# Sums of squares of the weight blocks on TensorE instead of ScalarE, for blocks 4 to 15 of a three-layer kernel

## The chip, the cores and the metric

The kernel runs on one core of a Trainium2 chip. The metric is the device time of one execution in microseconds; the time before is 1081.05 us, the median of three runs (1079.14 to 1084.92). The core has five engines with a queue of instructions each: TensorE (PE; its loads of weights are shown apart as PEld), VectorE (DVE), ScalarE (ACT), GpSimd (POOL) and SyncE (SP), which issues most transfers. Each engine takes its queue in the order in which the program lists it, and waits on semaphores for the others.

## The reference

Three layers follow each other: an attention between tokens and a small state, a dense layer with a squared Relu, and a layer of eight experts of which each token takes one.

```
scores = x @ state.T / 8;  a = softmax(scores);  xread = a @ state        # x: 8 batches, 8 heads, 512 x 64
scores2 = state @ x.T / 8; a2 = softmax(scores2); sread = a2 @ x          # state: 32 x 64 per head
x = concat(xread, sread) as 4608 tokens of 512
h = x @ w_in;  x = relu(h)**2 @ w_out                                     # w_in 512 x 2048, w_out 2048 x 512
expert = argmax over 8 of cosine(x, expert_emb) / tau, gate = its softmax
out = gate * (relu(x @ w1[expert]) @ w2[expert])                          # w1 512 x 1024, w2 1024 x 512
```

The inputs w_in and w_out come as float64, that is as words of 8 bytes, and the kernel decodes them to float32 itself.

## The kernel before

**Weights.** w_in and w_out are read in 16 blocks of 128 x 1024 numbers, numbered 0 to 15 in the order in, in, out, out, in, in, out, out and so on (`BLOCKS`). A block of w_in is 256 of its 2048 columns, a block of w_out 256 of its 2048 rows. Block 4 is the third of w_in, and 4 to 15 hold six of each. A raw block lies in one of a few places (`RAW_IN`) that is used again for later blocks: block 10 goes where block 6 lay, block 15 where 12 lay.

`to_f32` decodes a block in three steps. ScalarE turns the upper words into a float16 tile, the *top* (L915; two tiles named rec take turns). ScalarE or VectorE copies the top into float32 (L922 or L925), by which of the two the planner holds less loaded. VectorE sets the lower bits into it by a shift and an or (L928). Then the squares are summed. For w_in, `wi_scale` has ScalarE square the block into a tile pjk (L947), four matmuls against ones add over the rows (L955, into a bank of ps_u), and VectorE takes the maximum over columns (L961); for each pair of blocks that gives a power of two as scale (swi). For w_out, `wo_square` squares on ScalarE with a running sum (L1006); all eight sums are needed for the scale of w_out (L1028 and after).

The float16 products work on pairs of a high and a low part. `wi_split` and `wo_split` make them of the float32 blocks with the scales (L993 and L1054 on ScalarE, L317 on VectorE).

**The first tokens.** The kernel starts on tokens before all weights are there. For batch 0, `first_state_w` multiplies the state by float32 blocks as they come (L668) and splits the result (L677, L317). `up1` makes the hidden values in units u of 256 tokens and steps c = 0 to 7 of 256 columns (L1395 to L1397; below: Up c=0 to c=7); step c = 2k and 2k+1 needs the blocks 2k and 2k+1 of w_in and their scale. `hidden` applies Relu and square on ScalarE (L1348, L1352). `down1` multiplies unit 0 by w_out in float32 (L1458; Down c=0 to 7), later units in float16 (L1479 to L1481). Batch 1's attention begins meanwhile with sums of squares of its tokens and its state (L463, L465, L471).

**What sets the order.** The program is written by a planner: each piece of work is a thread with a priority, which yields the engine it needs next and a duration that the source assumes. `Plan.run` takes, over all threads, the step that can start first, then the one with the lower priority number, and each engine's queue is the order in which it took them. TensorE's banks of accumulation are rings of two (ps_u for sums and Up, ps_t for small products). At a priority of 1.3 to 5, a TensorE step counts as ready 1.75 us later than planned; the threads of the blocks have about 1.

Of the kernel before, what the change touches and what calls it, by code (L numbers as in the profile page):

```python
# [41 lines left out]
BW = DFF // NB  # L42
# [6 lines left out]
EASE = 1.0  # L49
LOADER = 9  # L50
AHEAD = 5
PRIO_A0 = 0.8
PRIO_A1 = 1.25
PRIO_S0 = 1.1
ATT = (0, 1, 2, B, 3, 4, 5, 6, 7)
XE = 2
# [168 lines left out]
def act(n):  # L225
    return "act", 0.1 + 0.83e-3 * n


def dve(n):
    return "dve", 0.09 + 1.045e-3 * n  # L230
# [10 lines left out]
def pe(k, n):  # L241
    return "pe", k * max(0.025, 0.0005 + n * 0.4205e-3)
# [3 lines left out]
def moe_kernel(  # L246
# [17 lines left out]
    nc = tc.nc  # L264
    ctx.enter_context(tc.manual_schedule())
    plan = Plan()
# [15 lines left out]
    att = ctx.enter_context(tc.tile_pool(name="att", bufs=1, side="right"))  # L282
# [54 lines left out]
    def load(dst, src, nbytes):  # L337
# [32 lines left out]
    smin, ismin = ends[:, 0:2], ends[:, 2:4]  # L370
# [23 lines left out]
    wi32 = [(wi_t[:, q + 1].rearrange("p h k f -> p (h k f)") if q < NB - 1 else  # L394
             wo[0].rearrange("p a k d -> p (a k d)")).bitcast(F32).rearrange("p (k f) -> p k f", k=4) for q in range(NB)]
# [5 lines left out]
    def ev(*key):  # L401
        return evs.setdefault(key, Ev(plan))
# [489 lines left out]
    top_slots = Ring(plan, 2)  # L892
    tops = [mg.tile([128, REC], F32, name=f"rec{k}", bufs=1)[:, :512].bitcast(BF16) for k in (4, 5)]

    def to_f32(n, dst, squares, squared):

        raw = raws.pop(n)
        slots = raw_in[RAW_IN[n]][0]
        over = [m for m in range(n) if RAW_IN[m] == "wo8"] if BLOCKS[n] in (("o", NB - 2), ("o", NB - 1)) else []
        if not W64:  # L900
            w = raw.bitcast(F32)
            plan.add(squares(w), plan.cur[1])
            for m in over:
                yield ev("read", m)
            yield dve2(1024)
            V.tensor_copy(dst, w)
        else:
            raw = raw.rearrange("p (n two) -> p n two", two=2)
            at = plan.now()
            yield top_slots  # L910
            plan.cur[2] = max(at, plan.now())
            k_t = top_slots.last()
            top = tops[k_t % 2]
            yield act(1024)
            nc.scalar.activation(out=top.bitcast(F16), in_=raw.bitcast(BF16)[:, :, 2], func=AF.Copy)  # L915
            at = plan.now()
            for m in over:
                yield ev("read", m)
            plan.cur[2] = max(at, plan.now())
            if plan.load("act") < plan.load("dve"):  # L920
                yield act(1024)
                nc.scalar.copy(dst, top)  # L922
            else:
                yield dve2(1024)
                V.tensor_copy(dst, top)  # L925
            top_slots.release(k_t)
            yield dve(1100)
            V.scalar_tensor_tensor(out=dst.bitcast(I32), in0=raw[:, :, 0], scalar=13, in1=dst.bitcast(I32),  # L928
                                   op0=ALU.logical_shift_right, op1=ALU.bitwise_or)
            plan.add(squares(dst), plan.cur[1])  # L930
            squared = ev("raw", n)
        plan.add(freed(n, slots, squared), plan.cur[1])

    def freed(n, slots, squared):
        yield squared
        ev("read", n).set()
        slots.release()

    wv = {}

    def wi_scale(q, w):
        at = plan.now()
        yield pjk_slots
        plan.cur[2] = max(at, plan.now())
        sq = att.tile([128, 4, BW], BF16, name="pjk")
        yield act(1024)
        nc.scalar.activation(out=sq, in_=w.rearrange("p (k f) -> p k f", k=4), func=AF.Square)  # L947
        ev("wisq", q).set()
        at = plan.now()
        yield u_slots  # L950
        plan.cur[2] = max(at, plan.now())
        p, k_h = ps_u.tile([128, 512], F32, name="u"), u_slots.last()
        yield pe(4, BW)
        for k in range(4):
            mm(p[:, 0:BW], lhsT=oneb, rhs=sq[:, k, :], start=k == 0, stop=k == 3)  # L955
        pjk_slots.release()
        if q // 2 not in wv:
            wv[q // 2] = small.tile([128, 2], F32, name="wv")
        v = wv[q // 2]
        yield dve(BW)  # L960
        V.tensor_reduce(out=v[:, q % 2:q % 2 + 1], in_=p[:, 0:BW], axis=X, op=ALU.max)  # L961
        u_slots.release(k_h)
        ev("wv", q).set()
        if q % 2:
            yield ev("wv", q - 1)
            qs = slice(q - 1, q + 1)
            yield tiny(5)
            w = small.tile([128, 4], F32, name="p2m")[:, 0:2]
            V.tensor_scalar(out=w, in0=v, scalar1=v[:, 0:1], scalar2=v[:, 1:2], op0=ALU.max, op1=ALU.max)
            v = w  # L970
            V.tensor_scalar(out=v, in0=v, scalar1=FLOOR, scalar2=None, op0=ALU.max)
            pow2(swi[:, qs], iswi[:, qs], v, 204)
            for a in (q - 1, q):
                ev("swi", a).set()
            yield ev("cg", 0)
            yield tiny(1)
            V.tensor_scalar(out=cgq[:, qs], in0=iswi[:, qs], scalar1=cg[:, 0:1], scalar2=None, op0=ALU.mult)
            ev("cgq", q // 2).set()

    def wi_block(n, q):  # L980
        yield ev("raw", n)
        yield from to_f32(n, wi32[q].rearrange("p k f -> p (k f)"), lambda a: wi_scale(q, a), ev("wisq", q))
        ev("wi32", q).set()
        plan.add(wi_split(q), PRIO_SPLIT)

# [11 lines left out]

    woacc = small.tile([128, NB], F32, name="woacc", bufs=1)

    def wo_square(q, w):  # L1000
        at = plan.now()
        yield pjk_slots
        plan.cur[2] = max(at, plan.now())
        jk = att.tile([128, 1024], BF16, name="pjk")
        yield act(1024)
        nc.scalar.activation(out=jk, in_=w, func=AF.Square, accum_out=woacc[:, q:q + 1])  # L1006
        pjk_slots.release()
        ev("wosq", q).set()

    def wo_block(n, q):  # L1010
        yield ev("raw", n)
        yield from to_f32(n, wo32[q].rearrange("p k d -> p (k d)"), lambda a: wo_square(q, a), ev("wosq", q))
        ev("f32", q).set()

    def weights():

        for n in range(1, len(BLOCKS)):
            if n == AHEAD:
                for t in range(2):
                    yield ev("asked", t)  # L1020
            yield from block(n)
            if n == LOADER:
                ev("w_in asked").set()
        for q in range(NB):
            yield ev("wosq", q)
            yield ev("swi", q)
        yield tiny(2)
        V.tensor_reduce(out=smin[:, 0:1], in_=swi, axis=X, op=ALU.min)  # L1028
        V.tensor_reduce(out=ismin[:, 0:1], in_=iswi, axis=X, op=ALU.max)
        yield from tensor_scale(woacc, smin[:, 1:2], ismin[:, 1:2])  # L1030
# [26 lines left out]
        split_lo(wo[q][:, 1], w, swo[:, q:q + 1], wo[q][:, 0])  # L1057
        ev("wo", q).set()

    def tensor_scale(acc, s, inv):  # L1060
# [12 lines left out]
        V.tensor_scalar(out=w, in0=p[:, 0:1], scalar1=FLOOR, scalar2=None, op0=ALU.max)  # L1073
        t_slots.release()
        pow2(s, inv, w, 204)

# [861 lines left out]
```

## Time and profile before

| | |
|---|---|
| Median of three runs | 1081.05 us |
| Profiled execution | 1085.53 us, span of its instructions 1083.7 us |
| TensorE matmuls busy | 1034.8 us, 95% of the span |
| VectorE busy | 669.9 us, 62% |
| ScalarE busy | 600.3 us, 55% |
| Granted TensorE clock, mean | 0.996 of 2.4 GHz |

Times in the rows are microseconds from the span's start unless marked ns. A row of the timeline shows the start, the time until the result is there, engine, line, operation, what it writes and reads and how often it stands there in a row, and in brackets how long the engine had been idle before and for whom. Matmuls overlap, so the time of one is longer than the distance to the next. A float32 matmul stands twice in the trace, and once in the program.

### The profile page before, as it was taken

Reading aid. Unit: us, or ns where it says so; the run is one execution under the profiler, and the core shown is the slowest. Engines: PE = TensorE matmul, PEld = TensorE weight load, DVE = VectorE, ACT = ScalarE, POOL = GpSimd, SP = SyncE. Lnnn points to the kernel's source line nnn. Section 1 sums busy time; section 2 is a strip of 40 time slices with the busy share of each in tenths; the row PEclk is TensorE's granted clock in tenths of the full one; section 3 lists DMA queues with packets and bytes.
Section 4 is the critical chain, followed back from the end, with each engine's and each line's share of the span. In section 5 each row is a group of like instructions: output and inputs, shape, how many; then the busy total and the mean of one; then the engine's idle time right before and its main releaser. Section 6 shows DMA issues by size and latency. Waiting matters only on the chain. (4 is left out here: it accounts for less than half of the span.)

```text
span 1083.7 us, 26223 instructions
## 1 busy us (share of the span) xinstructions
PE 1034.8 (95%) x10553; PEld 667.1 (62%) x10553; DVE 669.9 (62%) x1818; ACT 600.3 (55%) x1003; POOL 122.9 (11%) x149
## 2 busy tenths in 40 slices
PE   5789999899999999999999999999999999999998
PEld 4345465455565555656565666677676766767674
DVE  6779888778798877788887873465222222322222
ACT  6999898878887878879888783211111110101010
POOL 0000002002001001020010010321112111112111
PEclk9999999999999999999999999999999999999999
DMA  8843566755836655756766778834895767684792
GB/s 272 321 172 106 143 200 159 247 164 171 237 116 167 212 139 183 214 137 204 211 210 219 252 212 295 224 81 137 309 237 159 212 173 216 198 249 150 168 295 87
DMA packets 161599, 212.91 MB, mean 196 GB/s; under 512 B 112257, under 2 KB 115201, under 8 KB 156098
## 3 DMA queue, kind: packets, MB, share of 16 engines
q1 hardware_dynamic: 152722, 184.04, 58.1%
q0 software_dynamic: 8320, 27.08, 7.7%
q8 instruction: 84, 1.38, 0.5%
q14 instruction: 41, 0.34, 0.1%
q10 hardware_dynamic: 432, 0.08, 0.0%
HBM read 259.10 MB, written 51.68 MB: 287 GB/s over the span
## 5 line engine op out<-in xcount | busy, mean ns | idle before, releaser
L1745 ACT ACTIVATE r<-u 128x512 f32<-128x512 f32 x70 | 41.8, 597 | 323.3 <-PE u L1791 294.0
L1481 PE MATMUL d<-wo_t,g 128*128 128x512 f16 x512 | 194.1, 379 | 1.8 <-DVE g L1367 1.7
L1479 PE MATMUL d<-wo_t,g 128*128 128x512 f16 x512 | 194.0, 379 | 1.5 <-DVE g L1365 0.6
L1480 PE MATMUL d<-wo_t,g 128*128 128x512 f16 x512 | 194.0, 379 | 0.0
L1395 PE MATMUL u<-aT,sw 128*128 128x256 f16 x512 | 141.1, 276 | 7.7 <-ACT sw L677 4.3
L1397 PE MATMUL u<-aT,sw 128*128 128x256 f16 x512 | 140.8, 275 | 1.3 <-DVE sw L317 0.7
L1396 PE MATMUL u<-aT,sw 128*128 128x256 f16 x512 | 140.9, 275 | 0.5 <-issue 0.4
L1748 DVE CAST hh<-r 128x512 f16<-128x512 f32 x70 | 30.0, 429 | 137.3 <-ACT r L1745 135.8
L1348 ACT ACTIVATE r<-u,cg 128x512 f32<-128x512 f32 x128 | 87.5, 683 | 46.8 <-PE u L1397 22.8
L1759 DVE TENSOR_SCALAR o<-d,rec,wo_t 128x512 f32<-128x512 f32 x35 | 28.3, 809 | 107.6 <-PE d L1814 107.5
L1367 DVE TENSOR_TENSOR g<-r,g 128x512 f16<-128x512 f32 x128 | 87.7, 687 | 9.8 <-ACT r L1362 7.8
L1321 POOL DMA_INDIRECT rec_d<-rec,pi x34 | 37.6, 1105 | 494.0 <-DVE mt L774 91.2
L1814 PEld LDWEIGHTS <-hh 128*128 128x128 f16 (+1 forms) x688 | 54.6, 102 | 57.1 <-issue 0.4
L1481 PEld LDWEIGHTS <-g 128*128 128x128 f16 x512 | 50.0, 98 | 63.6 <-DVE g L1367 3.7
L1362 ACT ACTIVATE r<-r 128x512 f32<-128x512 f32 x128 | 80.2, 628 | 1.5
L1479 PEld LDWEIGHTS <-g 128*128 128x128 f16 x512 | 50.3, 98 | 49.2 <-DVE g L1365 1.1
L1480 PEld LDWEIGHTS <-g 128*128 128x128 f16 x512 | 50.1, 98 | 47.7 <-issue 0.9
L1789 PE MATMUL u<-xes,stage 128*128 128x128 f16 x448 | 76.1, 219 | 0.4 <-issue 0.4
L1790 PE MATMUL u<-xes,stage 128*128 128x128 f16 x448 | 76.1, 219 | 0.0
L1791 PE MATMUL u<-xes,stage 128*128 128x128 f16 x448 | 76.1, 219 | 0.0
L1395 PEld LDWEIGHTS <-sw 128*128 128x128 f16 x512 | 51.4, 100 | 33.0 <-issue 16.7
L1789 PE MATMUL u<-xes,xx 128*128 128x128 f16 x416 | 70.5, 219 | 0.0
(331 smaller groups left out, 2564.8 us busy)
## 6 DMA issues: line engine op xcount, KB each, us to landing
w_d<-he SPq DMA_DIRECT2D x128, 256.0 KB
g<-w_d SPq DMA_DIRECT2D x16, 2048.0 KB
wo_t<-w_d SPq DMA_DIRECT2D x16, 2048.0 KB
stage<-w_d SPq DMA_DIRECT2D x14, 2048.0 KB
he<-w_d SPq DMA_DIRECT2D x14, 2048.0 KB
xx<-w_d SPq DMA_DIRECT2D x13, 2048.0 KB
sw<-w_d SPq DMA_DIRECT2D x13, 2048.0 KB
stage<-in_w_dram SPq DMA_DIRECT2D x20, 1024.0 KB
```

Of the source, the lines that this page charges most:

```text
L1348: nc.scalar.activation(out=r, in_=ps, func=AF.Relu, scale=cg[:, g:g + 1] if u >= F32U else cgq[:, c:c + 1])
L1362: nc.scalar.activation(out=r, in_=r, func=AF.Square)
L1367: V.tensor_tensor(out=gl, in0=r, in1=gh, op=ALU.subtract)
L1395: mm(o, lhsT=hl[:, i, 0, fs], rhs=aT[:, i, :], start=i == 0, stop=False)
L1396: mm(o, lhsT=hl[:, i, 0, fs], rhs=aT[:, 2 + i, :], start=False, stop=False)
L1397: mm(o, lhsT=hl[:, i, 1, fs], rhs=aT[:, i, :], start=False, stop=i == 1)
L1479: mm(ps, lhsT=g_h[:, f, ts], rhs=w[:, 0, :], start=f == 0, stop=False)
L1480: mm(ps, lhsT=g_h[:, f, ts], rhs=w[:, 1, :], start=False, stop=False)
L1481: mm(ps, lhsT=g_l[:, f, ts], rhs=w[:, 0, :], start=False, stop=f == KF - 1)
L1789: mm(p[:, j, xs], lhsT=w[:, 0, k, fs], rhs=xe[:, k, xs], start=k == 0, stop=False)
L1790: mm(p[:, j, xs], lhsT=w[:, 0, k, fs], rhs=xe[:, 4 + k, xs], start=False, stop=False)
L1791: mm(p[:, j, xs], lhsT=w[:, 1, k, fs], rhs=xe[:, k, xs], start=False, stop=k == 3)
```

## The change

Blocks 4 to 15 (`GRAM`) no longer square their float32 form on ScalarE. As soon as a block's float16 top is there, TensorE multiplies each 128 x 128 piece of it by itself, eight matmuls into one 128 x 128 or two such sums; the sums of squares of the columns stand on the diagonals. VectorE multiplies by the unit matrix. For w_in a single matmul against ones in place of four then adds over the rows; for w_out VectorE adds over the columns. The top tile is given back after these products, and the raw place after the decoding. As tops are cut off below the exact number, the sums are multiplied by 1.14 and 1.13 before the power of two is taken. `PRIO_A1`, the priority of the attention threads of batches 1 to 8, is 1.24 for 1.25.

```
+GRAM = tuple(range(4, 16))
-PRIO_A1 = 1.25
+PRIO_A1 = 1.24
 # to_f32, after the top's conversion on ScalarE
+            gram = n in GRAM
+            if gram:
+                plan.add(squares(top, True), plan.cur[1])
...
+            if gram:
+                plan.add(topped(k_t, squared), plan.cur[1])
+            else:
+                top_slots.release(k_t)
+                plan.add(squares(dst, False), plan.cur[1])
+    def topped(k_t, squared):
+        yield squared
+        top_slots.release(k_t)
-    def wi_scale(q, w):
+    def wi_scale(q, w, gram):
+        if gram:
+            yield t_slots
+            p = ps_t.tile([128, 512], F32, name="t")[:, 0:BW].rearrange("p (c m) -> p c m", c=2)
+            w = w.rearrange("p (k c m) -> p k c m", k=4, c=2)
+            yield pe(8, 140)
+            for c in range(2):
+                for k in range(4):
+                    mm(p[:, c], lhsT=w[:, k, c], rhs=w[:, k, c], start=k == 0, stop=k == 3)
...
+        ks = 1 if gram else 4
+        if gram:
+            yield dve(BW)
+            V.tensor_tensor(out=sq.rearrange("p k (c m) -> p (k c) m", c=2), in0=p,
+                            in1=ident16.unsqueeze(1).to_broadcast([128, 2, 128]), op=ALU.mult)
+            t_slots.release()
...
-        yield pe(4, BW)
-        for k in range(4):
-            mm(p[:, 0:BW], lhsT=oneb, rhs=sq[:, k, :], start=k == 0, stop=k == 3)
+        yield pe(ks, BW)
+        for k in range(ks):
+            mm(p[:, 0:BW], lhsT=oneb, rhs=sq[:, k, :], start=k == 0, stop=k == ks - 1)
-    def wo_square(q, w):
+    def wo_square(q, w, gram):
+        if gram:
+            yield t_slots
+            yield pe(8, 140)
+            for c in range(8):
+                mm(p, lhsT=w[:, 128 * c:128 * c + 128], rhs=w[:, 128 * c:128 * c + 128], start=c == 0, stop=c == 7)
+            yield dve(128)
+            V.tensor_tensor(out=p, in0=p, in1=ident16, op=ALU.mult)
+            yield dve(128)
+            V.tensor_reduce(out=woacc[:, q:q + 1], in_=p, axis=X, op=ALU.add)
+            t_slots.release()
```

The planner lays all queues anew. On TensorE, where batch 0's first Up matmuls stand (L1395 before, L1442 after), these are the rows before, beginning with the last sum against ones for block 1; oneb are the ones, sw the state times w_in:

```order
L955 LDWEIGHTS oneb
L955 MATMUL u<-pjk,oneb 128x256
L1395 LDWEIGHTS sw
L1395 MATMUL u<-aT,sw 128x256
L1396 LDWEIGHTS sw
L1396 MATMUL u<-aT,sw 128x256
```

And these of the change, from the last of block 4's products (rec_128 is its top) to the first of block 5's (rec_129), ahead of Up:

```order
L962 LDWEIGHTS rec_128
L962 MATMUL t<-rec_128 128x128
L985 LDWEIGHTS oneb
L985 MATMUL u<-pjk,oneb 128x256
L962 LDWEIGHTS rec_129
L962 MATMUL t<-rec_129 128x128
```

The sums for blocks 4 and 5 stood behind the first Up matmuls and now stand before them, with a wait for VectorE between the two groups of products.

On ScalarE, from block 10's top (rec_128<-he) to block 11's and batch 1's first squares (L463, of its tokens; L465, of its state, some rows further on), before, beginning two rows ahead of it:

```order
L915 ACTIVATE rec_129<-stage 128x1024
L993 ACTIVATE wi<-wi,swi 128x1024
L915 ACTIVATE rec_128<-he 128x1024
L947 ACTIVATE pjk<-wi 128x1024
L1348 ACTIVATE r<-u,cgq 128x512
L993 ACTIVATE wi<-wi,swi 128x1024
L1352 ACTIVATE g<-r 128x2x2x128
L1348 ACTIVATE r<-u,cgq 128x512
L947 ACTIVATE pjk<-wi 128x1024
L1352 ACTIVATE g<-r 128x2x2x128
L463 ACTIVATE xx,ss<-xx 128x1024
L915 ACTIVATE rec_129<-wo_t 128x1024
```

The same piece of the change, where the top is L916, the copy L926, the Relu L1395, batch 1's squares L464 and L466:

```order
L916 ACTIVATE rec_128<-he 128x1024
L1023 ACTIVATE wi<-wi,swi 128x1024
L926 CAST wo_t<-rec_128 128x1024
L1395 ACTIVATE r<-u,cgq 128x512
L464 ACTIVATE xx,ss<-xx 128x1024
L1399 ACTIVATE g<-r 128x2x2x128
L464 ACTIVATE xx,ss<-xx 128x1024
L1395 ACTIVATE r<-u,cgq 128x512
L916 ACTIVATE rec_129<-wo_t 128x1024
L1399 ACTIVATE g<-r 128x2x2x128
L678 ACTIVATE sw<-S_521,swi 128x512
L466 ACTIVATE xx,ss<-stt 128x4x64
```

The squares (L947) are gone, a split and a copy stand between block 10's top and the Relu, and the squares of batch 1's state have two rows between them and block 11's top. Before there were six: the second square of batch 1's tokens, the squares of two blocks of w_out, two tops and a split.

## Rows read from the trace of the kernel before

**Rows 1.** The page's busy times: engine, us, share of the span, instructions.
```profile
PE 1034.8 (95%) x10553; PEld 667.1 (62%) x10553; DVE 669.9 (62%) x1818; ACT 600.3 (55%) x1003; POOL 122.9 (11%) x149
```

**Rows 2.** Stretches of 15 us: busy time (instructions) by engine, clock, DMA share, GB/s.
```profile
45.00:60.00 15.00, 12.46 (x79) 6.64 (x78) 9.84 (x12) 12.53 (x18) 0.38 (x2) 0.89 1.00 390
60.00:75.00 15.00, 12.07 (x79) 6.28 (x78) 12.05 (x37) 14.11 (x21) 0.18 (x1) 0.89 0.30 105
```

**Rows 3.** Timeline of TensorE, 28 to 80 us: start, us, engine, line, operation.
```profile
28.96 0.40 PE L1395 MATMUL u<-aT,sw 128*128 128x256 f16 x1 [3.85 <-ACT sw L677]
...
39.19 7.03 PE L1458 MATMUL d<-wo_t,g 128*128 128x512 f32 x16
...
51.38 0.61 PE L955 MATMUL u<-pjk,oneb 128*128 128x256 bf16 x4 [2.54 <-ACT r L1348]
...
53.81 4.40 PE L1458 MATMUL d<-wo_t,g 128*128 128x512 f32 x8
58.04 0.60 PE L955 MATMUL u<-pjk,oneb 128*128 128x256 bf16 x4
58.48 3.60 PE L1458 MATMUL d<-wo_t,g 128*128 128x512 f32 x8
64.00 0.39 PE L471 MATMUL t<-ss,one 128*128 128x3 f32 x2 [1.92 <-ACT xx L465]
...
65.52 1.01 PE L955 MATMUL u<-pjk,oneb 128*128 128x256 bf16 x4 [1.01 <-ACT pjk L947]
66.32 0.42 PE L1395 MATMUL u<-aT,sw 128*128 128x256 f16 x1
...
68.99 0.66 PE L668 MATMUL S<-wi,sthl 64*32 64x256 f32 x16
...
72.04 7.03 PE L1458 MATMUL d<-wo_t,g 128*128 128x512 f32 x16
```

**Rows 4.** Timeline of ScalarE, 30 to 64 us.
```profile
30.41 1.12 ACT L915 ACTIVATE rec<-g 128x1024 f16<-128x1024 bf16 x1
...
48.69 1.12 ACT L915 ACTIVATE rec<-he 128x1024 f16<-128x1024 bf16 x1 [1.75 <-DMA he<-in_w_out_dram]
...
50.66 0.67 ACT L1348 ACTIVATE r<-u,cgq 128x512 f32<-128x512 f32 x1
...
63.42 0.43 ACT L465 ACTIVATE xx<-stt 128x256 bf16<-128x256 f32 x1
```

**Rows 5.** Timeline of SyncE's queue: the issue of block 10's transfer.
```profile
43.52 0.41 SPq L339 DMA_DIRECT2D he<-in_w_out_dram  x1
```

**Rows 6.** Groups by line and form, 20 to 85 us: busy us, mean ns | idle before.
```profile
L1006 ACT ACTIVATE pjk<-wo_t 128x1024 bf16<-128x1024 f32 x8 | 8.4, 1053 | 1.1 <-ACT xx L463 0.7 <-DVE wo_t L928 0.2
...
L922 ACT CAST wo_t<-rec 128x1024 f32<-128x1024 bf16 x5 | 5.2, 1037 | 0.0
...
L961 DVE TENSOR_REDUCE wv<-u 128x1 f32<-128x256 f32 x7 | 3.0, 424 | 7.6 <-PE u L955 7.5
...
L925 DVE CAST wo_t<-rec 128x1024 f32<-128x1024 bf16 x4 | 2.8, 692 | 2.6 <-ACT rec L915 2.6
...
L1006 ACT ACTIVATION_READ_ACCUMULATOR pjk<-wo_t 128x1 f32 x8 | 1.5, 191 | 0.0
```

**Rows 7.** Timeline of TensorE: first matmul of one expert tile, and first behind it.
```profile
764.86 0.22 PE L1789 MATMUL u<-xes,xx 128*128 128x128 f16 x1
...
770.22 0.59 PE L1814 MATMUL d<-he,hh 128*128 128x512 f16 x2
```

**Rows 8.** TensorE's waits, 0 to 300 us: us in total, times, longest.
```profile
PE u L955 <- ACT pjk L947: 2.5, 4, 1.0
```

**Rows 9.** Timeline of TensorE, 100 to 200 us: three of its waits.
```profile
116.35 0.39 PE L1481 MATMUL d<-wo_t,g 128*128 128x512 f16 x1 [1.23 <-DVE g L1367]
...
192.68 0.26 PE L1242 MATMUL t<-en,xr 128*128 128x16 f16 x4 [1.05 <-DMA xr<-rec]
...
196.63 0.20 PE L809 MATMUL t<-he,xx 128*128 128x64 f16 x1 [1.09 <-DVE xx L317]
```

More of the change, by code (lines that the diff above doesn't have):

```diff
@@ L901, in to_f32 @@
             w = raw.bitcast(F32)
-            plan.add(squares(w), plan.cur[1])
+            plan.add(squares(w, False), plan.cur[1])
             for m in over:
@@ L915, in to_f32 @@
             nc.scalar.activation(out=top.bitcast(F16), in_=raw.bitcast(BF16)[:, :, 2], func=AF.Copy)
-            at = plan.now()
+            converted = plan.now()
+            gram = n in GRAM
+            if gram:
+                plan.add(squares(top, True), plan.cur[1])
             for m in over:
                 yield ev("read", m)
-            plan.cur[2] = max(at, plan.now())
+            plan.cur[2] = max(converted, plan.now())
             if plan.load("act") < plan.load("dve"):
@@ L925, in to_f32 @@
                 V.tensor_copy(dst, top)
-            top_slots.release(k_t)
             yield dve(1100)
@@ L929, in to_f32 @@
                                    op0=ALU.logical_shift_right, op1=ALU.bitwise_or)
-            plan.add(squares(dst), plan.cur[1])
+            if gram:
[3 more added lines that the diff above has]
+                plan.add(squares(dst, False), plan.cur[1])
             squared = ev("raw", n)
         plan.add(freed(n, slots, squared), plan.cur[1])
+    def topped(k_t, squared):
+        yield squared
+        top_slots.release(k_t)
     def freed(n, slots, squared):
@@ L939, in moe_kernel @@
     wv = {}
-    def wi_scale(q, w):
+    def wi_scale(q, w, gram):
+        if gram:
+            at = plan.now()
+            yield t_slots
+            plan.cur[2] = max(at, plan.now())
+            p = ps_t.tile([128, 512], F32, name="t")[:, 0:BW].rearrange("p (c m) -> p c m", c=2)
[4 more added lines that the diff above has]
+                    mm(p[:, c], lhsT=w[:, k, c], rhs=w[:, k, c], start=k == 0, stop=k == 3)
+            ev("wisum", q).set()
         at = plan.now()
@@ L944, in wi_scale @@
         plan.cur[2] = max(at, plan.now())
-        sq = att.tile([128, 4, BW], BF16, name="pjk")
-        yield act(1024)
-        nc.scalar.activation(out=sq, in_=w.rearrange("p (k f) -> p k f", k=4), func=AF.Square)
+        ks = 1 if gram else 4
+        sq = att.tile([128, 4, BW], BF16, name="pjk")[:, :ks]
+        if gram:
[3 more added lines that the diff above has]
+            t_slots.release()
+        else:
+            yield act(1024)
+            nc.scalar.activation(out=sq, in_=w.rearrange("p (k f) -> p k f", k=4), func=AF.Square)
+            ev("wisum", q).set()
         ev("wisq", q).set()
@@ L970, in wi_scale @@
             v = w
-            V.tensor_scalar(out=v, in0=v, scalar1=FLOOR, scalar2=None, op0=ALU.max)
+            V.tensor_scalar(out=v, in0=v, scalar1=1.14, scalar2=FLOOR, op0=ALU.mult, op1=ALU.max)
             pow2(swi[:, qs], iswi[:, qs], v, 204)
@@ L981, in wi_block @@
         yield ev("raw", n)
-        yield from to_f32(n, wi32[q].rearrange("p k f -> p (k f)"), lambda a: wi_scale(q, a), ev("wisq", q))
+        yield from to_f32(n, wi32[q].rearrange("p k f -> p (k f)"), lambda *a: wi_scale(q, *a), ev("wisum", q))
         ev("wi32", q).set()
@@ L998, in moe_kernel @@
     woacc = small.tile([128, NB], F32, name="woacc", bufs=1)
-    def wo_square(q, w):
+    def wo_square(q, w, gram):
+        if gram:
+            at = plan.now()
+            yield t_slots
+            plan.cur[2] = max(at, plan.now())
+            p = ps_t.tile([128, 512], F32, name="t")[:, 0:128]
+            yield pe(8, 140)
+            for c in range(8):
+                mm(p, lhsT=w[:, 128 * c:128 * c + 128], rhs=w[:, 128 * c:128 * c + 128], start=c == 0, stop=c == 7)
+            ev("wosum", q).set()
+            yield dve(128)
[3 more added lines that the diff above has]
+            t_slots.release()
+            ev("wosq", q).set()
+            return
         at = plan.now()
@@ L1007, in wo_square @@
         pjk_slots.release()
+        ev("wosum", q).set()
         ev("wosq", q).set()
@@ L1011, in wo_block @@
         yield ev("raw", n)
-        yield from to_f32(n, wo32[q].rearrange("p k d -> p (k d)"), lambda a: wo_square(q, a), ev("wosq", q))
+        yield from to_f32(n, wo32[q].rearrange("p k d -> p (k d)"), lambda *a: wo_square(q, *a), ev("wosum", q))
         ev("f32", q).set()
@@ L1029, in weights @@
         V.tensor_reduce(out=ismin[:, 0:1], in_=iswi, axis=X, op=ALU.max)
-        yield from tensor_scale(woacc, smin[:, 1:2], ismin[:, 1:2])
+        yield from tensor_scale(woacc, smin[:, 1:2], ismin[:, 1:2], 1.13)
         yield tiny(3)
@@ L1058, in wo_split, with tensor_scale @@
         ev("wo", q).set()
-    def tensor_scale(acc, s, inv):
+    def tensor_scale(acc, s, inv, margin=1.0):
         v = small.tile([128, 1], F32, name="fv")
@@ L1072, in tensor_scale @@
         yield tiny(4)
-        V.tensor_scalar(out=w, in0=p[:, 0:1], scalar1=FLOOR, scalar2=None, op0=ALU.max)
+        V.tensor_scalar(out=w, in0=p[:, 0:1], scalar1=margin, scalar2=FLOOR, op0=ALU.mult, op1=ALU.max)
         t_slots.release()
```

## The prediction

> **What bounds the kernel now.** I read the busy shares first. TensorE's matmuls are busy for 1034.8 of 1083.7 us [rows 1], so the whole program can lose at most the 48.9 us in which TensorE has no matmul, and every matmul that is added counts unless it falls into such a gap. Next I read the table by stretches. From 45 to 75 us ScalarE works 12.5 and 14.1 of every 15 us, VectorE 9.8 and 12.1, TensorE 12.5 and 12.1 [rows 2]: TensorE is short of 5.5 us while ScalarE is nearly full. The granted clock reads 0.89 in both stretches. Its two levels are 1.2 and 2.4 GHz, so a missing 0.11 is some 3.4 us at 1.2 GHz in each: the twelve matmuls of 256 columns from 66.32 to 68.99 us take 0.22 us each, where the four from 58.04 to 58.48 take 0.11 [rows 3].
>
> Then the timeline of TensorE [rows 3] shows which waits these are. It has nothing from 48.8 to 51.38 us (2.54 us, for a Relu on ScalarE), and waits 1.92 us before 64.00 (for the squares of batch 1's state) and 1.01 us before 65.52 (for the squares of block 12). The two half-clock pieces come right behind the first and the third of these waits; each costs up to half its 3.4 us, 1.7 us. Together 2.54 + 1.92 + 1.01 + 2 x 1.7 = 8.9 us of what the change could give back. ScalarE's own timeline [rows 4] says why the Relu is late: at 48.69 us ScalarE has just waited 1.75 us for block 10, whose transfer was issued at 43.52 us [rows 5], and the Relu (50.66) is queued behind it.
>
> **The change, part by part.** ScalarE loses 12 squares of 1.05 us (six of blocks of w_in, six of w_out) and six reads of an accumulator of 0.19 us: 12 x 1.05 + 6 x 0.19 = 13.7 us. The planner spends some of it: in the new order ScalarE makes 11 of the 16 copies of a top into float32 where it made 7, 4 x 1.04 = 4.2 us more; net 9.6 us less, nearly all of it between 32 and 79 us. VectorE loses 4 copies x 0.69 = 2.8 us and gains six products of 128x256 and six products and six sums of 128x128. Nearest to the first is the maximum over 128x256 in PSUM, 0.42 us; for the others I halve the part that grows with the columns and take 0.28. That is 6 x 0.42 + 12 x 0.28 = 5.9 us, net 3.1 us more (2 to 5, as the small ones take 0.2 to 0.42) [rows 6].
>
> TensorE gains 12 x 8 = 96 products of 128x128 in float16, each with weights of its own. The trace has this form in the second layer: one tile's 96 such matmuls run from 764.86 to 770.22 us, 5.36 us, or 0.056 each [rows 7]. At 1.2 GHz they take twice that, so 5.4 to 10.7 us; I take 5.4, since most fall behind 39 us, where the clock is up. It loses 6 x 3 = 18 matmuls against ones of 0.11 us (four from 58.04 to 58.48), 2.0 us. Net 3.4 us more work on the engine that is the bound.
> The Trainium skill's "TensorE: Matmul & The Clock Gate", section "Back-to-back issue gap", puts a sustained stream of weight load and matmul at about 81 ns for 128 columns, against 56 for a lone gap. By it the products would take 96 x 0.081 = 7.8 us and the forecast below would be 2.4 us higher. The trace disagrees: 96 pairs in a row keep 56 ns here.
>
> Each of the 12 groups of products waits for its top (ScalarE) and a free bank of ps_t, and each of the six sums against ones for a product on VectorE. TensorE takes its queue in order, so whatever stands behind waits too. Of such a wait the trace shows the old form: four waits for ScalarE's squares, 2.5 us in all, 0.6 us each [rows 8]. From below it is 0 (the top is there), from above 0.6 us times 18. I don't take a mean: I walk the new queues over the places where TensorE lost time, with durations from the rows.
>
> *Blocks 4 and 5.* In the old queue the first Up matmuls start at 28.96 us. In the new one a group for block 4, a single sum against ones, and a group for block 5 stand ahead. Block 5's top starts at 30.41 on ScalarE [rows 4] and ends about 31.5; eight products at 1.2 GHz take 0.9 us. So Up starts at about 32.4, 3.4 us later. About 2.1 us of that is still there when the float32 Down matmuls start (41.3 against 39.19). Its cover is the empty 2.54 us before 51.38, so I cost it at nothing; without that cover it costs 2.1 us.
>
> *Block 10.* Its transfer is behind the same queue and the same constants, so its top can't start before 48.69. In the new order ScalarE reaches it at about 48.1 and has it at 49.7. Its eight products stand in front of the second half of Up matmul c=2 and wait for that. Then: products 50.2, Up 50.9, the sums for the first batch's state (blocks 8, 9) to 51.9, Up c=3 from the Relu (52.4) to 53.7. The old queue reaches the same place at 53.81 [rows 3]. So here the change gains nothing although the 2.54 us wait is gone, as TensorE has also done 56 products by then; but no wait of that length is left ahead of it, so I expect no half clock here.
>
> *Batch 1's state.* ScalarE goes on from 52.4 us without the three squares that stand between that Relu and batch 1's state in the old order (3 x 1.05 + 2 x 0.19 = 3.5 us [rows 6]). It reaches the squares of batch 1's state at about 57.8 us, against 63.42 [rows 4]. TensorE: Down c=2 54.0 to 57.5 (8 matmuls take 3.44), block 11's products 57.9, the state's sums 58.4, Down c=3 61.9, block 12's products 62.3 (its top is out at 59.1), Up c=4 63.6. The old Up c=4 ends at 68.99: 5.4 us earlier, for the waits of 1.92 and 1.01 and the second half clock have gone.
>
> *To block 15.* Blocks 13, 14 and 15 add three groups (1.35 us) and lose 0.7 us of sums. I get Down c=4 at 67.2 against 72.04, block 15's products at about 71.1, and the end of Down c=5 at 74.6 against 78.9 (72.04 + 16 x 0.43). **The lead at that point is 4.3 us.** From there TensorE is full until 112 us in the old trace, and I let the lead stand: what the freed ScalarE does there is hidden by TensorE's own work. The new priority of attention (1.24 for 1.25) changes ties against other threads and moves no work of its own; I cost it at nothing, covered by TensorE's queue, and at 2.5 us either way (one wait like that before 51.38) if that cover is gone.
>
> The profiled execution took 1085.53 us (span 1083.70 and 1.83 around it). 1085.5 - 4.3 = 1081.2 for such an execution. The median of three is 1081.05, 4.5 us below the profiled one; on it the sum is 1081.05 - 4.3 = **1076.8 us**.
>
> **Rivals.**
> *Waits in order (slower).* The 18 new places where TensorE's queue holds for a top or for VectorE cost what the old ones did, 0.6 us each, 11 us. With 3.4 us of work and all 8.9 us recovered that is +5.5 us, about 1086.6; if the second half clock stays, 1088.3. It decides from 18 w + 3.4 = 8.9, w = 0.3 us. For it: the planner gives these groups no margin, and VectorE is busier. Against it: in the walk only the groups of blocks 5 and 10 and the first single sum hold the queue. Place: the groups of blocks 8 to 15.
> *Freed ScalarE beside the path (no change).* TensorE gets back only what the products cost, 3.4 us, or the lead of 4.3 us is used up between 112 and 200 us, where VectorE and transfers already make TensorE wait (1.23 us before 116.35, 1.05 before 192.68, 1.09 before 196.63 [rows 9]): about 1081. For it: the new order differs from here to 660 us, and VectorE has 3.1 us more to do. Against it: that work lies before 80 us.
> *More than the lead.* ScalarE comes out of the weights up to 9.6 us earlier, and those three waits (3.4 us) go too: 4.3 + 3.4 = 7.7 us, 1073.4. For it: the engine that is late there is freed. Against it: two of the three waits are for VectorE and one for a transfer.
> *It doesn't do what it says.* The products belong to the path for weights of 8 bytes; the tops of 128x1024 in the trace [rows 4] show that this path runs. The factor 1.14 on the sum can only move a power of two, which costs no time. I give this nothing.
>
> **How the numbers follow.** Forecast (1074 to 1080) 0.45; more than the lead 0.20; no change 0.22; waits in order 0.13. About 0.5%, 5.4 us, is what a measurement of this kernel can tell from no change: below 1075.6 is faster, above 1086.5 slower. Of the forecast's own range somewhat under half lies below 1075.6, as 4.3 is near the border: 0.20, and with the 0.20 of the second, faster 0.40. The slower rival's middle is at the border and its upper end beyond, and I count it all as slower: 0.13. The rest, 0.47, is no change. The range of 8 in 10 leaves out 0.13 above and some 0.05 below: 1070.5 to 1083.5. It holds the doubled price of the products (+5.4 us on 1076.8) but for its last part.
>
> **What would show it.** Right: 96 products of about 0.06 us; no wait of over 1.5 us and no half-clock piece from 45 to 75 us; ScalarE's squares of batch 1's state near 58 us; block 10's products near 49.8 us; Down c=4 and c=5 ending near 74.6 us. Wrong: an idle column of the products' lines that sums to over 5 us (waits in order), products at 0.08 us or more, a half-clock piece that stays, or a lead at 75 us that is not in the span (lost between 100 and 660 us).

## The result, and the profile after

The changed kernel takes 1093.64 us, the median of seven runs (1088.61 to 1096.57), against 1081.12 us for seven of the kernel before: a ratio of 1.0105, 95% interval 1.0078 to 1.0133. I had forecast 1076.8 us. It is slower, and outside my range. The profiled execution took 1096.57 us, with a span of 1094.8 against 1083.7, 11.1 us more.

The first 75 us went nearly as I had walked them. The table by stretches, in the same columns as [rows 2], shows that TensorE is idle for 0.03 us from 45 to 75 us and runs at the full clock:

```profile
45.00:60.00 15.00, 14.97 (x106) 7.96 (x105) 13.91 (x32) 14.94 (x21) 0.00 (x0) 1.00 1.00 391
60.00:75.00 15.00, 15.00 (x124) 9.21 (x123) 14.46 (x37) 12.68 (x17) 0.37 (x2) 1.00 0.21 74
```

TensorE's timeline of the changed kernel, the places of [rows 3]:

```profile
31.57 1.03 PE L962 MATMUL t<-rec 128*128 128x128 bf16 x8 [1.63 <-ACT rec L916]
32.40 0.42 PE L1442 MATMUL u<-aT,sw 128*128 128x256 f16 x1
...
39.06 0.62 PE L1038 MATMUL t<-rec 128*128 128x128 bf16 x8
39.52 3.65 PE L1505 MATMUL d<-wo_t,g 128*128 128x512 f32 x8
...
48.18 0.62 PE L1038 MATMUL t<-rec 128*128 128x128 bf16 x8
...
60.65 0.27 PE L1442 MATMUL u<-aT,sw 128*128 128x256 f16 x1
...
65.78 3.60 PE L1505 MATMUL d<-wo_t,g 128*128 128x512 f32 x8
69.21 0.61 PE L1038 MATMUL t<-rec 128*128 128x128 bf16 x8
69.66 3.65 PE L1505 MATMUL d<-wo_t,g 128*128 128x512 f32 x8
73.15 0.27 PE L1442 MATMUL u<-aT,sw 128*128 128x256 f16 x1
```

The first Up matmul starts at 32.40, block 10's products at 48.18, and Down c=5 ends at 73.15 where the old one ended at 78.9: a lead of 5.8 us. Eight products take 0.46 us (39.06 to 39.52), the pace of [rows 7]. The page's busy line answers [rows 1]:

```profile
PE 1040.8 (95%) x10631; PEld 673.3 (61%) x10631; DVE 673.0 (61%) x1833; ACT 591.0 (54%) x988; POOL 119.2 (11%) x149
```

To see where the lead went I took from the timelines, for every matmul, the distance to the next one, less what that distance is for its shape when nothing is late (the lower quartile over the traces). What is left over is TensorE's lost time, half clock included. Summed between the same matmuls of each program (D: Down matmuls by their number in the trace, the 64 records of the float32 ones first; U: Up matmuls of the expert layer), in us; the runs e7 to e18 come in the next section, and chip 13 is one on which every kernel is faster:

```
                       to D96 to D432 to D816 to D1056 to D1440 to U200 to U3888  end    sum
end of stretch about     110    245     398     495      638     712     1053
before                  36.2   22.1    15.3    11.6      8.3     1.8    46.3     5.5   147.0
changed                 26.8   19.3    19.6    11.4     12.1     6.8    48.7    10.1   154.7
e7  (before, padded)    35.8   20.4    14.2     9.5      8.4     1.7    45.3     9.3   144.6
e17 (changed, two mended)28.6  21.2    18.2    11.4     12.5     1.7    45.7     5.7   144.9
e18 (order kept, padded) 31.3  21.5    14.5     9.4      9.3     1.6    44.3     6.0   138.0
e12 (changed, chip 13)  27.8   19.0    14.2     9.7      8.7     8.4    37.1    10.2   135.1
```

Changed less before: 12.2 us won up to 245 us; then 4.3, 3.8, 5.0, 2.4 and 4.6 us lost in five places; together 7.7 more lost, and 11.1 - 7.7 = 3.4 us of added work. (The trace of the kernel before is of an execution 4.5 us over its median; e7, with the same order, had lost 147.0 - 144.6 = 2.4 us less, its stop near the end included.)

**The handover to the expert layer** (to U200). The expert weights are read, scaled, split and written back to memory (w_d<-he) in the background of everything before, by `experts`; the expert layer then loads them as first weights of its tiles (stage, he, xx, sw) on SyncE, and transposes the gathered records (xes<-rec) there too. SyncE's queue in the kernel before, at this place:

```profile
650.84 3.92 SPq L339 DMA_DIRECT2D w_d<-he  x4
656.93 0.36 SPq L1695 DMA_DIRECT2D stage<-w_d  x1
658.98 0.34 SPq L1695 DMA_DIRECT2D he<-w_d  x1
...
667.24 0.35 SPq L1695 DMA_DIRECT2D xx<-w_d  x1
683.47 1.93 SPq L1735 DMA_TRANSPOSE xes<-rec  x1
```

and in the changed one:

```profile
649.78 11.35 SPq L340 DMA_DIRECT2D w_d<-he  x10
663.15 0.36 SPq L1742 DMA_DIRECT2D stage<-w_d  x1
665.24 0.34 SPq L1742 DMA_DIRECT2D he<-w_d  x1
...
682.50 3.02 SPq L1782 DMA_TRANSPOSE xes<-rec  x2
688.44 1.24 SPq L1279 DMA_TRANSPOSE xr<-rec  x1
691.82 0.35 SPq L1742 DMA_DIRECT2D xx<-w_d  x1
```

Two things differ: the write-back ends 6 us later (its last issue is at 660.80 for 654.43), and xx<-w_d stands behind two transposes that wait for a gather, 24.6 us later. TensorE stops in the first tile, then waits for xx, and goes on at half clock (0.11 from one matmul to the next, where it was 0.056):

```profile
698.87 0.22 PE L1838 MATMUL u<-xes,stage 128*128 128x128 f16 x1 [0.98 <-issue]
...
702.23 0.29 PE L1836 MATMUL u<-xes,xx 128*128 128x128 f16 x1 [2.13 <-DMA xx<-w_d]
...
702.52 0.31 PE L1836 MATMUL u<-xes,xx 128*128 128x128 f16 x1
702.63 0.31 PE L1837 MATMUL u<-xes,xx 128*128 128x128 f16 x1
```

**The end.** TensorE stops in the middle of a tile, for nothing that the program waits for, and the clock is at its lower level for the 3.4 us behind:

```profile
1063.44 0.19 PE L1836 MATMUL u<-xes,g 128*128 128x64 f16 x1
1066.34 0.20 PE L1837 MATMUL u<-xes,g 128*128 128x64 f16 x1 [2.71 <-issue]
```

The transfers between 1063.4 and 1066.3 us hold one packet of queue 8 (kind, packets, MB, share), on which TensorE's instructions arrive: 85 packets of 16,384 bytes in this execution. There is none in the 10 us before.

```profile
q8 instruction: 1, 0.02, 2.2%
```

### The profile page after: what moved, and what is told of

Its sections match the earlier page's. It is cut to its first block, busy times and chain, and to the rows that moved or that the text cites. A ratio compares the mean times of both kernels' runs of the same rounds, so it can differ in the third digit from the quotient of the medians.

```text
span 1094.8 us, 26358 instructions
## 1 busy us (share of the span) xinstructions
PE 1040.8 (95%) x10631; PEld 673.3 (61%) x10631; DVE 673.0 (61%) x1833; ACT 591.0 (54%) x988; POOL 119.2 (11%) x149
## 5 line engine op out<-in xcount | busy, mean ns | idle before, releaser
L1442 PE MATMUL u<-aT,sw 128*128 128x256 f16 x512 | 140.3, 274 | 5.1 <-ACT r L1395 4.9
L1395 ACT ACTIVATE r<-u,cg 128x512 f32<-128x512 f32 x128 | 87.3, 683 | 47.3 <-PE u L1444 30.8
L1368 POOL DMA_INDIRECT rec_d<-rec,pi x34 | 36.2, 1064 | 510.7 <-DVE rec L1364 181.0
L1526 PEld LDWEIGHTS <-g 128*128 128x128 f16 x512 | 50.4, 98 | 48.7 <-DVE g L1412 2.0
L1836 PE MATMUL u<-xes,xx 128*128 128x128 f16 x416 | 72.1, 222 | 2.5 <-DMA xx<-w_d 2.1
L1838 PE MATMUL u<-xes,xx 128*128 128x128 f16 x416 | 72.0, 221 | 0.4 <-issue 0.4
```

The source lines that it names most:

```text
L1395: nc.scalar.activation(out=r, in_=ps, func=AF.Relu, scale=cg[:, g:g + 1] if u >= F32U else cgq[:, c:c + 1])
L1442: mm(o, lhsT=hl[:, i, 0, fs], rhs=aT[:, i, :], start=i == 0, stop=False)
L1526: mm(ps, lhsT=g_h[:, f, ts], rhs=w[:, 0, :], start=f == 0, stop=False)
L1836: mm(p[:, j, xs], lhsT=w[:, 0, k, fs], rhs=xe[:, k, xs], start=k == 0, stop=False)
L1838: mm(p[:, j, xs], lhsT=w[:, 1, k, fs], rhs=xe[:, k, xs], start=False, stop=k == 3)
```

## The experiments

The runs stand on five chips by the record's numbers. On chips 14 (e1 to e4), 10 (e5 to e8) and 8 (e16 to e18) the kernel before takes 1079 to 1080 us, as it did for the result (1081); I call these the first kind. On chips 12 (e9 to e11) and 13 (e12 to e15) it takes 1072 to 1073 us: the second kind. Ratios are to the kernel before on the same chip, with 95% intervals.

**e1, the order of SyncE at the handover.** In the kernel before:
```
-                        yield ev("moe1") if name == "w2" else ev("cum", NXT - 1)
+                        yield ev("moe1") if name == "w2" else ev("xe", 1)
```


> The kernel before, with SyncE's queue at the handover to the expert layer set as it stands in the changed kernel: the load of the second expert tile's first weights (xx<-w_d) goes behind the first two transposes of gathered records (xes<-rec), not ahead of them. No products of tops, the old priority. Theory A (the queue's order at the handover is what makes the changed kernel slower): xx<-w_d is issued after about 688 us (before: 667.24), lands some 10 us later, TensorE waits for it around 700 us and then runs at half clock for about 3.4 us; the time goes from 1081.1 to 1085 to 1089 us (4.1 to 7.7 us, the slips that the two traces show between the last Down matmuls and the third expert half tile). Rival B (the products themselves cost it: 6.0 us more TensorE work and new waits for the tops): no change, 1081 us.

1084.16 us, 1.0047 (1.0029 to 1.0065). xx<-w_d was issued at 687.78, and the handover lost 5.3 us for 1.8. The price is that of theory A's lower end, but its mechanism was not there: the trace has no wait for xx<-w_d. TensorE stopped three times for 0.7 to 1.1 us between 688 and 691 us, in Up matmuls of the first tile (stage) and for nothing that the profile names, and then ran at half clock. Nor was SyncE's queue all that moved: the planner also set the first Up matmuls ahead of the last Down matmuls (684.6 us for 693.6) and dealt TensorE's and VectorE's queues anew from there to 758 us. So the new order at the handover costs some 4 us; by which of its parts isn't shown.

**e2, the priority alone.** In the kernel before:
```
-PRIO_A1 = 1.25
+PRIO_A1 = 1.24
```

> The kernel before with the priority of the later batches' attention at 1.24 for 1.25, and nothing else. Theory A: the planner's order on SyncE at the handover turns to that of the changed kernel by this number alone, so 1085 to 1089 us with a wait for xx<-w_d near 700 us. Rival B (the products): 1081 us, no such wait. Rival C (the priority costs early, in the attention stages up to 420 us, and the handover only shows it): slower by 3 us or more before 650 us already.

1086.60 us, 1.0068 (1.0046 to 1.0091), with the changed kernel's order at the handover (xx<-w_d at 691.76) and this wait:
```profile
PE u L1789 <- DMA xx<-w_d: 1.7, 1, 1.7
```
So the number that I had costed at nothing brings 6.6 us, by the middle values more than half of the loss; the order differs from the old one from 147 us on. Whether C has a part in it the traces leave open: between D432 and D816 e2 loses 3.0 us more than the kernel before, but up to D1440 its lost times add up to about 1 us less than those of the kernel before, and 4 us more than those of e7, whose order is that of the kernel before.

**e3, the products alone.** In the changed kernel:
```
-PRIO_A1 = 1.24
+PRIO_A1 = 1.25
```

> The changed kernel with the priority at the old 1.25: products of tops for blocks 4 to 15, and nothing else of the change. Theory A: xx<-w_d is issued ahead of the transposes again (near 668 us), no TensorE wait over 1 us from 650 to 720 us, and the lead of about 4 us that the walk gave the changed kernel at 75 us is in the time: 1077 us (1074 to 1081). Rival B: 1090 to 1095 us, as with 1.24.

1094.42 us, 1.0137 (1.0116 to 1.0159): theory A fails as I put it. xx<-w_d does stand ahead of the transposes, but the planner has dealt a third order: the write-back ends at 667.7, stage<-w_d is issued at 670.30 and xx<-w_d at 674.21, and TensorE waits for records that land behind them:
```profile
PE u L1836 <- DMA xes<-rec: 6.6, 1, 6.6
```
So each half of the change deals an order that loses, and the two losses don't add (0.68% and 1.37%, together 1.05 to 1.22%).

**e4, xx ahead in the changed kernel.**
```
-                        yield ev("moe1") if name == "w2" else ev("cum", NXT - 1)
+                        yield ev("moe1") if name == "w2" else ev("cum", SEEN - 1)
```


> The changed kernel, whole, with one condition of a load relaxed: the first weights of the second expert tile (xx<-w_d) may be asked for once the records of the first 24 token tiles are counted, not the first 32, which puts the load ahead of the transposes on SyncE. Theory A: the wait for xx<-w_d and the half clock after it go; the time falls from 1093.6 by 7.7 us or more, to 1078 to 1086 us (the low end if the 2.7 us stop at 1066 us of the profiled execution is a chance of that execution). Rival B: no change, 1090 to 1095 us.

1090.46 us, 1.0105 (1.0081 to 1.0128). The wait for xx went, and 1.7 us for xes<-rec came; the handover still lost 5.2 us. By the ratios it is no faster than the changed kernel (1.0105, 1.0122 and 1.0112 in its three groups). The place of xx is not the whole of it. Formed from e3 and e4: the late end of the preparation (theory G). And in all three kernels with products TensorE stopped for 2.6 to 2.9 us within one matmul of the same place near the end, and in none of the others (theory F).

**e5, the changed kernel again.**

> The changed kernel as it is, once more, so that the others of this group are held against it on one chip, and for a second profile of it. If the stop of 2.7 us in the last half tile before the end (1066 us) and the half clock after it belong to the program and not to one execution, they are there again, some 100 Up matmuls before the last; if they are chance, they are gone or elsewhere.

1093.56 us, 1.0122 (1.0095 to 1.0148); the stop is there, 3.3 us. It belongs to the program.

**e6, the changed kernel with 51 empty matmuls; e7, the kernel before with 77.** In `first_attention`, ahead of TensorE's first matmul:
```
+        for _ in range(51):          # e7: 77
+            mm(p[:, 128:129], lhsT=oneb, rhs=oneb[:, 0:1], start=True, stop=True)
```


> The changed kernel with 51 empty matmuls (102 instructions with their weight loads) at TensorE's start, where it waits for the first load. TensorE's program is then 256 instructions longer than that of the kernel before (154 of the products and 102), and 256 instructions of 64 bytes are one of the 16,384-byte packets in which the trace shows its instructions arriving. Theory F (the stop near the end comes from where the borders of these packets fall in the fast last half tile, not from the data): the stop of 2.7 us and the half clock behind it go, about 4.5 us less than the changed kernel. Rival: no effect, or the small cost of the padding.

> The kernel before with 77 empty matmuls (154 instructions, as many as the products add to TensorE) at TensorE's start, and nothing else. Theory F: a stop of 2 to 3 us some 100 Up matmuls before the last, which the kernel before did not have, and about 4.5 us more time. Rival: no effect.

e6: 1088.35 us, 1.0068 (1.0047 to 1.0089), 5.2 us under e5. e7: 1085.02 us, 1.0046 (1.0028 to 1.0064), 4.7 us over the kernel before. The one lost the stop, the other gained it:
```profile
1051.98 0.21 PE L1792 MATMUL u<-xes,g 128*128 128x64 f16 x1 [2.38 <-issue]
```
Both as theory F expected. e7's queues are those of the kernel before in every other row, and e6's those of the changed one. Counted through the traces (TensorE's weight loads, matmuls and waits), the stop stands behind instruction 20,928 or 20,929 in all ten traces that have one of over 2 us, whatever order the kernel has and on both kinds of chip.

**e8, earlier preparation.** In the changed kernel:
```
-PRIO_E1 = 2.2
+PRIO_E1 = 1.9
```

> The changed kernel with the preparation of the expert weights (scale, split, write back) ranked ahead of more of the other work once attention is done (priority 1.9 for 2.2). Theory G (the handover is late because the preparation ends late: its last write w_d<-he is issued at 660.8 us against 654.4 before, and the first expert loads wait for it): the last write comes 6 to 8 us sooner, the loads stage, he and xx with it, the handover loses 2 to 3 us instead of 7 to 10, and the time falls by 5 to 8 us below the changed kernel's. Rival (the queue's order alone): not under 1089 us, as the run in which xx alone was put ahead.

1091.80 us, 1.0087 (1.0056 to 1.0118), six runs from 1084.85 to 1094.00. The write-back ended at 652.7 and the handover lost 2.4 us; but the profiled run, at 1093.34 us among the longer ones, has a new wait, again with half clock behind it:
```profile
820.92 0.23 PE L1836 MATMUL u<-xes,g 128*128 128x64 f16 x1 [3.31 <-DMA xes<-rec]
```
The handover is as G has it; the time is inconclusive.

**e9 and e10, the products with the order of before kept.** In the kernel before: the products and the diagonal in 11 of the 12 blocks, with nothing told to the planner (e10: and 54 empty matmuls). In the traces every other row of TensorE, ScalarE, VectorE and SyncE stands where it stood before.
```
+            if n in GRAM and t_slots.ready():
+                t_slots.take()
+                gram = ps_t.tile([128, 512], F32, name="t")[:, ...]   # and eight matmuls from top
             top_slots.release(k_t)
...
         yield act(1024)                                  # the planner still counts the square
+        if gram is None:
             nc.scalar.activation(out=sq, ..., func=AF.Square)
+        else:
+            V.tensor_tensor(out=sq..., in0=gram..., in1=ident16..., op=ALU.mult)
```


> The kernel before with the products put in and its order kept: in 11 of blocks 4 to 15 TensorE's products and VectorE's diagonal stand where the ScalarE square stood, but the planner is still told of the square, so that every other instruction of every engine stands where it stood before; old priority. (The twelfth block finds no free PSUM bank and keeps its square.) Theory H (what the changed kernel loses after 110 us comes from the order that the planner dealt anew, and from the code border near the end, not from the products' work): the handover and the attention stages lose no more than before, the early walk wins some 4 us net of 3.4 us of added TensorE work, and the stop near the end is there (147 more instructions): about 1080 us, against 1093 of the changed kernel. Rival B (the products' own work and waits): 1088 us or more.

> The same with 54 empty matmuls (108 instructions) at TensorE's start, so that the program is 254 instructions longer than before, about one packet. Theory H with F: the stop near the end is gone too, and the time is 1075 to 1078 us, under the kernel before (1080). Rival B: 1084 us or more. If the early walk's gain does not outlast the stages between (because TensorE waits there for something else than the work before it): 1080 us or a little more.

e9: 1072.32 us, 1.0004 (0.9986 to 1.0022). e10: 1071.37 us, 0.9987 (0.9974 to 1.0000). Rival B falls by the ratios; the times in the expectations were for the first kind of chip. e9 has the stop (2.9 us) and e10 hasn't, but e10 is only 1.0 us faster, within the intervals.

**e11, e13 and e17, both mended.** The changed kernel with `PRIO_E1 = 1.9` and the 51 empty matmuls; **e12 and e16**, the changed kernel beside it.

> The changed kernel with the earlier preparation of the expert weights (priority 1.9) and the 51 empty matmuls together. If the two causes add: about 5 us under the run with the earlier preparation alone (1091.8), 1085 to 1087 us; what is left over the kernel before is then the waits of the new order in the attention stages (about 4 us each in 250 to 400 us and 490 to 640 us). If they are one and the same: 1088 to 1092 us.

> The changed kernel as it is, beside the next three on one chip: the measure for what they undo. 1.0 to 1.3% over the kernel before, with the stop of 2 to 3 us in the last half tile.

> The changed kernel with the earlier preparation of the expert weights and the 51 empty matmuls, again, with the changed kernel itself on the same chip. If the late preparation and the code border are the whole of what was lost: 9 to 12 us under the changed kernel, within 3 us of the kernel before; if another cause of 4 us or more is left: more than 4 us over the kernel before.

> The changed kernel once more, to tell which chip this group runs on: 1.0 to 1.3% over the kernel before as in the first groups, or 0.1% as in the last.

> The changed kernel with earlier preparation and padding. On a chip where the changed kernel is 12 us over the kernel before: 7 us or more under it if the two causes add (5.2 from the padding, 2 or more from the preparation); 5 us if the padding alone does it.

Second kind: e12 1075.54 us, 1.0014 (0.9994 to 1.0035); e11 1072.52, 1.0000 (0.9986 to 1.0014); e13 1071.20, 0.9984 (0.9970 to 0.9997), 4.3 us under e12 where I expected 9 to 12. There the changed kernel is hardly slower, against my expectation. First kind: e16 1093.19 us, 1.0112 (1.0095 to 1.0129); e17 1085.39, 1.0051 (1.0036 to 1.0066), 7.8 us less, as expected if the two add. e17's SyncE at the handover is that of the kernel before again:
```profile
655.93 0.36 SPq L1744 DMA_DIRECT2D stage<-w_d  x1
658.02 0.34 SPq L1744 DMA_DIRECT2D he<-w_d  x1
...
664.86 1.14 SPq L1744 DMA_DIRECT2D xx<-w_d  x1
683.86 1.26 SPq L1784 DMA_TRANSPOSE xes<-rec  x1
```

**e14, e15 and e18, the order kept, again** (e14 and e18 padded).

> The products with the order of the kernel before kept and 54 empty matmuls, again, with the changed kernel on the same chip. Theory H: within 2 us of the kernel before, on either side, and 11 us or more under the changed kernel. Rival B (the products' work): 4 us or more over the kernel before.

> The products with the order kept and no padding: by theory F the stop in the last half tile is there, and the time 3 to 5 us over the run with the padding.

> The products with the order kept and the padding. On a chip where the changed kernel is 12 us over the kernel before: not above the kernel before, if the products cost nothing there either (theory H); 4 us or more above it by rival B.

e14: 1069.40 us, 0.9970 (0.9958 to 0.9982); e15: 1073.25, 0.9997 (0.9981 to 1.0013), 3.9 us over e14, with a stop of 3.3 us that e14 has not. First kind, e18: 1078.34 us, 0.9986 (0.9973 to 0.9998), 14.9 us under the changed kernel beside it and 7.1 us under e17. With the padding this version is 1 to 4 us under the kernel before (e10, whose interval reaches 1, e18 and e14); without it, it takes the same time (e9, e15).

## Why the prediction was wrong

*The walk to 75 us* was right, and a little short: a lead of 5.8 us for 4.3. The walk had taken what stands ahead of Down c=0 slower than it ran (39.52 for 41.3), and so block 10's products came at 48.18 for 49.7. ScalarE squared batch 1's state at 55.86, where I had 57.8 and [rows 4] 63.42:
```profile
55.86 0.41 ACT L466 ACTIVATE xx<-stt 128x256 bf16<-128x256 f32 x1
```
No half-clock piece was left. Of the 8.9 us recoverable, the table shows 9.4 up to 110 us.

*The work* was right: 3.4 us more on TensorE, as the lost times and the span give it (the page's busy time, with modelled ends of matmuls, is 6.0 us more); ScalarE 9.3 us less (I had 9.6), VectorE 3.1 more (3.1), by the page's busy times.

*Waits in order* came to 3.9 us before the products (I had set 5 us as the sign) and 2.3 us before the sums against ones, more than the 2.5 us of [rows 8], but not where that rival had them. The lines of the products and of their sum against ones, by form from 20 to 85 us (busy, mean ns | idle before):
```profile
L962 PE MATMUL t<-rec 128*128 128x128 bf16 x48 | 4.5, 249 | 3.9 <-ACT rec L916 3.9
...
L1038 PE MATMUL t<-rec 128*128 128x128 bf16 x48 | 4.1, 235 | 0.0
L985 PE MATMUL u<-pjk,oneb 128*128 128x256 bf16 x10 | 2.9, 354 | 2.3 <-DVE pjk L971 2.3
```
They are three waits ahead of the first Up matmul, where the old queue had 3.85 us [rows 3] and the walk had put the new ones; behind it, in the groups of blocks 8 to 15, there is none. That rival had the right direction, but the loss is in other places.

*The failing step* is the sentence "From there TensorE is full until 112 us in the old trace, and I let the lead stand", with the one on the priority, "I cost it at nothing". I had taken the end of the walk for the end of the change. But products and priority are both inputs of the planner, and it dealt the order anew up to 764 us (behind that the two programs agree); the priority alone costs 6.6 us (e2). In the new order the background preparation of the expert weights, which has the lowest rank on ScalarE and VectorE, fell back (its 33rd write is issued at 335.76 us for 288.55, its last 6 us late). TensorE lost 6.8 us at the handover for 1.8, and the lead was gone: U200 starts at 715.0 us, before at 710.8. What the runs showed in place of the lead, on the first kind of chip:

- about 5 us for the border in TensorE's program (e6, e7; on the second kind 3.9 in e15 and 1.0 in e9). Order and data have no part in it: 154 more instructions (78 matmuls with their weight loads, two waits less) moved a border of the instruction packets into a tile whose matmuls follow each other in 0.03 us;
- 2.5 to 5 us of TensorE's time at the handover, for the new order there (e1, e2; e17's handover loses 1.7 us for the 6.8 of e16, and for the 4.3 and 4.2 of e5 and e6, which have the changed kernel's order too). In time this repair isn't shown: e17 is 1.8 us under e6 by the ratios, within the intervals, and e8 is inconclusive;
- what is left of e17, 6 us over the kernel before and 7.1 over e18. Beside e18, on the same chip and padded too, the table has it: e17 loses 3.0 us less up to 245 us, 8.9 us more from 245 to 638 us and 1.2 more behind. So it lies in the waits of the new order between 245 and 638 us. Which of them would have to go wasn't tried; one in the changed kernel from 243 to 396 us, 2 times, 2.3 us at most (before: 1.1 us in all):
```profile
PE t L472 <- ACT xx L466: 4.6, 2, 2.3
```

e18 shows that it was the order: the products with the old order lose nothing there. It also shows that the products in that order bring little: a lost time of 31.3 us up to 110 us for 36.2, less their own work. They stand there in places that the planner did not choose for them; the first group holds TensorE's queue until 31.5 us for its top:
```profile
PE t L937 <- ACT rec L918: 5.4, 1, 5.4
```
The rest of the 9.4 us came with the new order, and so did its price.

*Open*: why the same program loses less on the second kind of chip (e12: 14.2 and 8.7 us to D816 and D1440, for 19.6 and 12.1, and most of all 37.1 in the expert layer, for 48.7). After 110 us, the traces of the first kind have 17 to 34 places where 0.4 to 0.7 us are lost between two matmuls, those of the second 8 to 14; what makes them wasn't tried. The new order itself costs less on the second kind: e13 is 1.8 us over e14, where on the first e17 is 7.1 over e18. The wait at 820 us in e8 isn't settled either. And the kernel before was profiled in an execution 4.5 us over its median; of the same order, e7 was 6 us ahead of it at 640 us, so single stretches are compared here only where several traces agree.

## What to carry to other kernels

Where a planner deals the order, a change of a duration or a priority is a change of the whole queue: follow the lowest-ranked background work to the next point where the bounding engine depends on it, and look at the order of every queue there, before letting a lead stand. To learn what a change is worth by itself, put it in with the old order kept. Before believing a per cent, shift the program by some empty instructions and look whether it stays, and measure on more than one chip.

## What the runs showed of the hardware

TensorE's instructions arrive in packets of 16,384 bytes (84 in the kernel before, 85 in the changed one), and at one border TensorE stopped for 2.4 to 3.3 us with no wait for another engine or a transfer, and lost some 1.7 us more by 3.4 us of half clock behind it. In the changed kernel a packet came during the stop, 11.4 us after the one before; in e6, with 102 more instructions ahead, one came at 1056.7 us, 4.0 us before TensorE was at instruction 20,928, and no stop of over 0.7 us was left:
```profile
PE u L1839 <- issue: 0.7, 1, 0.7
```
The Trainium skill's "Runtime: NRT & Kernel Launch", section "Instruction fetch mechanics", has programs refilled in blocks of 16 KiB, 256 instructions, and the cost of a border mostly hidden. The trace agrees on the 16 KiB; a border that cost 3.9 to 5.2 us in e6, e7 and e15 (1.0 in e9) is not hidden. The distance between packets doesn't explain it: e6's came 11.8 us after the one before it, and one in the kernel before 12.4 us, both without a stop of over 0.7 us. What makes this packet late is open. That 102 empty instructions at the start can take such a stop away, and 154 bring one, was new to me.
